# The last chunk of an FNet-and-GLU kernel: closing the sums one group early and making the last group in row form

## The chip, the cores and the metric

The kernel runs on one core of one Trainium2 chip. The metric is the device time of one execution in microseconds (us), lower is better. The profile's times are on one profiled execution's clock; its span runs from the first to the last instruction. The engines are PE (TensorE, with PEld for its weight loads), DVE (VectorE), ACT (ScalarE), POOL (GpSimd) and SP (SyncE, which here only issues DMAs).

## The reference

```python
# x: (8, 3008, 256) float32
X = np.fft.fft(x, axis=1)
X = np.fft.fft(X, axis=2)
y = X.real.reshape(8 * 3008, 256)

gate = 1.0 / (1.0 + np.exp(-(y @ w_gate)))      # w_gate, w_val: (256, 1536)
val = y @ w_val
out = gate * val @ w_out                        # w_out: (1536, 256), out: (24064, 256)
```

## The kernel before

The Fourier transform over the sequence is made with tables of cosines and sines, by folds of x on POOL and DVE and products on PE. The transform over the features is merged into the weights of gate and value (`G1`, `G2`). Rows k and S - k of a sequence come out of the same products, as sum and difference, so the main loop handles two mirrored rows at a time.

The main loop runs over batches (8), chunks of at most 252 row pairs (6 per batch, the last of 246), and the 12 blocks of 128 hidden features. One step of it is a slot: 576 slots. Three slots make a group, four groups a chunk; the last group has the number 191. In a slot, `front_a` and `front_b` make the gate and value products into a PSUM bank `pf`; `seed` and `part` put the middle feature in and take a copy; `gate_a` and `gate_b` apply the sigmoids and multiply, which leaves in `h` a tile of 128 hidden features by n row pairs, twice (for the row and its mirror). All of it is laid out with features on the partitions.

The product with `w_out` doesn't multiply plainly. It is a bilinear scheme that saves products: per group, three feature blocks, three thirds of the 2n rows and two halves of the 256 outputs are multiplied with 15 products instead of 18 (`PRODUCTS`), from sums of blocks of `h` (`sf`, made by POOL in `gate_b`, L653: 13 per group) and sums of blocks of `w_out` (`wf`, made once at the start). `back` issues the 15 products of a group in three parts of five, five slots behind the front; they add up over the four groups of a chunk in five PSUM banks, `PO`, three blocks of R = 2n/3 columns in each. As soon as a bank has its last product in the fourth group, it is copied to the tile `c` (L677, on ACT or DVE).

`finish` then forms the outputs: 20 sums of blocks of `c` (`C_SUMS` and `C_LAST`, line L700), DVE transposes in blocks of 32 by 32 (`flip`, L710), since here the output features are on the partitions, and stores in runs of 64 features, 256 bytes (`store`, L719 and L723). For an ordinary chunk these steps are put on a list, `later`, and are taken from it two or three per slot beside the next chunk. In the last chunk nothing follows: they come straight after the last product, six of the sums go to POOL, the blocks of the fifth bank are read from PSUM without a copy, and the 16 stores alternate between the queues of SP and ACT.

The order on each engine is that of the program text. DMAs are issued by SP and ACT in order, and an instruction that waits holds up what stands behind it in its queue.

At the start the weights are loaded into tiles that later serve other ends. The last four feature blocks of `w_out` pass through tile `x4`, which then takes x of the next batches (L148); `weight_join` (L310) on POOL is the last step of a weight's conversion, `forms` makes the blocks of `wf` from it. `mirror_x` copies x of the next batch into a mirrored layout in DRAM (`xr`; L160, L164, L169), and `e_rows` (L583) loads a broadcast row `ek` for each chunk.

Of the kernel before, what the change touches and what calls it, by code (L numbers as in the profile page):

```python
# [6 lines left out]

F32 = mybir.dt.float32
I32 = mybir.dt.int32
# [43 lines left out]
NQ = 6  # L53
# [23 lines left out]
OUT = (3, 12)  # L77
# [4 lines left out]
def kernel(  # L82
# [10 lines left out]
    nc = tc.nc  # L93
    B, _, _, _, D = xf.shape
    F = moe_w_gate.shape[1]
    P = 128
    S = out.shape[0] // B
    M = S // 2
    NK = M + 1
# [3 lines left out]
    NPR = NFT // 2  # L103
    NG = NFT // 3
    CH = 252
    NB = 1 + max(b // 3 for b in PLACE)
    WC = 256
    HD = D // 2
    TB = 32
# [9 lines left out]
    xp = ctx.enter_context(tc.tile_pool(name="xp", bufs=1))  # L119
    pqp = ctx.enter_context(tc.tile_pool(name="pqp", bufs=2))  # L120
    dram = ctx.enter_context(tc.tile_pool(name="dram", bufs=1, space=bass.MemoryType.DRAM))
# [5 lines left out]
    sp = ctx.enter_context(tc.tile_pool(name="sp", bufs=2))  # L127
    cp = ctx.enter_context(tc.tile_pool(name="cp", bufs=2))
    op = ctx.enter_context(tc.tile_pool(name="op", bufs=1))
# [3 lines left out]
    def mm(o, l, r, start, stop):  # L133
        nc.tensor.matmul(o, l, r, start=start, stop=stop, skip_group_check=True)  # L134

    def bank(name, other=None):
        if other is not None:
            return pso.tile([P, 512], F32, name=name, tag=f"po{other}")
        return psx.tile([P, 512], F32, name=name, tag="x")
# [46 lines left out]
    zero = dram.tile([2, 1, D], F32, name="zero")  # L186
    table = const.tile([2, 1], F32, name="table")
    ed = dram.tile([B, NK + 1], F32, name="ed")

    def load_table(t, nq):  # L190
        for q in range(0, NQ, nq):
            yield nc.sync.dma_start(out=ST[0][0:NP, t, q : q + nq], in_=stab[:, t, q : q + nq])
# [119 lines left out]
    WO, parts_ = {}, []  # L312

    def weight_use(j, other=None):
        w, c = jobs[j]
        if w == 2:
            WO[c] = WS.pop(j)
            for g in range(NG):
                if (3 * g + 2) // 2 == c:
                    parts_.extend(forms(g))  # L320
        else:
            merge(WS.pop(j), w, c, other)
# [244 lines left out]
    chunks = [(k0, min(CH, -(-(NK - k0) // 3) * 3)) for k0 in range(0, NK, CH)]  # L567
    assert NK <= chunks[-1][0] + chunks[-1][1] <= NK + 1 and NFT == 12
    groups = [(b, c, g) for b in range(B) for c in range(len(chunks)) for g in range(NG)]
    H, SF, EK = {}, {}, {}  # L570

    def cut(i):
        b, c, _ = groups[i // 3]
        k0, n = chunks[c]
        f = i % NFT
        return PQE[b], slice(k0, k0 + n), n, f, slice(f * P, (f + 1) * P)
# [41 lines left out]
    def front_b(i):  # L618
        (_, qk, *_), ks, _, _, fs = cut(i)
        for g in range(2):  # L620
            mm(PF[i][:, g], G2[:, g, fs], qk[:, ks], False, True)
# [15 lines left out]
    def block(p, i):  # L637

        R = 2 * chunks[groups[p][1]][1] // 3
        return H[p][:, i % 3, i // 3 * R : (i // 3 + 1) * R] if i < 9 else SF[p][:, i - 9, 0:R]  # L640

    def gate_b(i):

        n = cut(i)[2]
        p, fh = i // 3, i % 3
        z, h, pf = Z.pop(i), H[p], PF.pop(i)
        nc.vector.tensor_tensor(h[:, fh, 0:n], h[:, fh, 0:n], pf[:, 1], op=ALU.mult)  # L647
        nc.scalar.activation(pf[:, 0], z[:, 0], AF.Sigmoid)  # L648
        nc.vector.tensor_tensor(h[:, fh, n:], pf[:, 0], z[:, 1], op=ALU.mult)  # L649
        if fh == 1:  # L650
            SF[p] = sp.tile([P, 8, 2 * CH // 3], F32, name="sf", tag="sf")
        for dst, a, b, op in H_SUMS.get(fh, ()):
            nc.gpsimd.tensor_tensor(block(p, dst), block(p, a), block(p, b),  # L653
                                    op=(ALU.subtract, ALU.add)[op])
# [3 lines left out]
    C = {}  # L658

    def back(p, part):  # L660

        b, c, g = groups[p]
        n = chunks[c][1]
        R = 2 * n // 3
        last = p == len(groups) - 1
        if part == 0 and g == 0:
            PO[:] = [pso.tile([P, 2 * WC], F32, name=f"po{t}", tag=f"po{t}") for t in range(NB)]
        for at_, (hb, wb) in list(enumerate(PRODUCTS))[part * 5 : part * 5 + 5]:
            t, j = divmod(PLACE[at_], 3)
            mm(PO[t][:, j * R : (j + 1) * R], wf[:, g, wb], block(p, hb), g == 0 and at_ % 3 == 0,  # L670
               g == NG - 1)
            if g == NG - 1 and at_ % 3 == 2:
                if t == 0:
                    C[0] = cp.tile([P, 10 * WC], F32, name="c", tag="c")
                    nc.gpsimd.memset(C[0][:, 15 * R : 15 * R + 40], 0.0)
                if not (last and t == NB - 1):
                    (nc.vector.tensor_copy if t == 1 or t == 3 and not last else nc.scalar.copy)(  # L677
                        C[0][:, 3 * t * R : 3 * (t + 1) * R], PO[t][:, 0 : 3 * R])
        if part == 2:
            del H[p], SF[p]  # L680
            if g == NG - 1:
                finish(b, c, last)

    def finish(b, c, last):
        k0, n = chunks[c]
        R = 2 * n // 3
        more = k0 + n > NK
        nb = -(-n // TB)
        t = C.pop(0)
        queues = (nc.sync, nc.scalar) if last else (nc.sync,)  # L690
        os_ = []

        new = set()

        def sum_(dst, a, b, op, engine=nc.vector):

            there = lambda i: last and i >= 3 * (NB - 1) and i not in new
            v = [PO[NB - 1][:, (i - 3 * NB + 3) * R : (i - 3 * NB + 4) * R] if there(i) else
                 t[:, i * R : (i + 1) * R] for i in (a, b)]
            engine.tensor_tensor(t[:, dst * R : (dst + 1) * R], *v, op=(ALU.subtract, ALU.add)[op])  # L700
            new.add(dst)

        def flip(s, h):
            if not os_:

                full = (sp.tile([P, 8 * (2 * CH // 3)], F32, name="os", tag="sf") if last else
                        op.tile([P, NK + 1], F32, name="os", tag="os"))
                os_.append(full[:, 0 : 4 * WC].rearrange("p (s b h j) -> p s b h j", s=2, h=2, j=TB))
            c0 = OUT[h] * R + (n + more if s else 0)
            nc.vector.transpose(os_[0][:, s, 0:nb, h, :], t[:, c0 : c0 + nb * TB])  # L710

        def store(s):
            m, r0 = (min(n, M - k0), b * S + k0) if s == 0 else (
                n - (k0 == 0) - more, b * S + S - k0 - n + 1 + more)
            full = m // TB
            for a in range(4):
                ps = slice(a * TB, (a + 1) * TB)
                cs = slice(a * 2 * TB, (a + 1) * 2 * TB)
                queues[a % len(queues)].dma_start(  # L719
                    out=out[r0 : r0 + full * TB, cs].rearrange("(b t) d -> t b d", t=TB),  # L720
                    in_=os_[0][ps, s, 0:full].rearrange("p b h j -> p b (h j)"))
                if m > full * TB:
                    queues[a % len(queues)].dma_start(out=out[r0 + full * TB : r0 + m, cs],  # L723
                                      in_=os_[0][a * TB : a * TB + m - full * TB, s, full].rearrange(
                                          "p h j -> p (h j)"))

        def add(f):
            if last:
                f()
            else:  # L730
                later.append(f)
        for x, e in C_SUMS:
            if x[0] == 7:
                add(lambda: flip(0, 0))
                add(lambda: (flip(0, 1), store(0)))
            add(lambda x=x, e=e: sum_(*x, engine=(nc.vector, nc.gpsimd)[last and e]))
        add(lambda: sum_(*C_LAST))
        add(lambda: flip(1, 1))
        add(lambda: (flip(1, 0), store(1)))


# [61 lines left out]
    def at(i, *fs):  # L803
        side.setdefault(i, []).extend(fs)
# [14 lines left out]
    i0 = NFT  # L819
    count = 3 * len(groups)  # L820
# [16 lines left out]
    for b in range(B - 1):  # L837
# [17 lines left out]
        if b < B - 2:  # L855
            at(g0 + 1, lambda b=b: load_x(b + 2))
            for i, f in zip(calm(s0 if b else 3 * i0), mirror_x(b + 2)):
                at(i, f)

    for i in range(count):  # L860
        front_a(i)
        if N1 <= i < NFT:
            part(i)
        if i:
            gate_a(i - 1)
        if not N1 <= i < NFT:
            part(i)
        if i0 <= i + 1 < count:
            seed(i + 1)
        if i:  # L870
            gate_b(i - 1)
        todo = pre.pop(i, []) + use.pop(i, [])
        for f in [parts_.pop(0)] + todo if parts_ else todo + [lambda: parts_ and parts_.pop(0)()]:
            f()
        if i >= 5:
            back((i - 5) // 3, (i - 5) % 3)
        front_b(i)
        n = 3 if i >= count - 8 else 2 + i % 2
        for f in later[0:n]:
            f()  # L880
        del later[0:n]
        for f in side.pop(i, []):
            f()
# [55 lines left out]
```

## Time and profile before

| what | value |
|---|---|
| runs | 1955.82, 1955.66, 1949.49 us; median 1955.66 |
| span of the profiled execution | 1953.1 us (no other time of its own is given for it) |
| granted TensorE clock, mean | 0.995 |
| PE busy | 1915.7 us, 98% |
| DVE, ACT, POOL busy | 1457.9, 1332.5, 1598.4 us |
| chain that ended last, by engine | PE 92%, DVE 4%, DMA 2%, ACT 1% |
| chain from 1934 us on, by line | PE po L134 33.5%, DVE c L700 18.2%, DVE os L710 5.6%, PE pf L134 4.1%, ACT c L677 2.9% |

The table's shares of the chain say what the end of the program was waiting for, step by step back from its last instruction. All matrix products are recorded by one helper, L134; they are told apart by the tile that they write: `pf` for the gate and value products, `po` for the products with `w_out`. A matrix product in float32 shows as two instructions.

### The profile page before, as it was taken

The page shows a single profiled execution, that of the slowest core. Times are in us where ns is not written, and L with a number is a line of the kernel's source. Part 1 is how long each engine was busy: PE and PEld are TensorE (multiplying, and loading weights), DVE is VectorE, ACT ScalarE, POOL GpSimd, SP SyncE. Part 2 cuts the span into 40 slices and gives each one's busy share as a digit, 9 for nine tenths or more (in the row PEclk, how much of TensorE's full clock was granted, in tenths as well). Part 3 has the DMA queues.
Part 4 walks back from the last instruction along what each step waited for, and adds up shares of the span by engine and source line. Part 5 has one row for each costly group of instructions (what it writes and reads, how often), then busy time and mean ns, then how long its engine had stood idle before and what let it go on. Part 6 is the DMA issues. An engine that isn't in the chain of part 4 may idle for free.

```text
span 1953.1 us, 34554 instructions
## 1 busy us (share of the span) xinstructions
PE 1915.7 (98%) x11252; PEld 1788.2 (92%) x11252; DVE 1457.9 (75%) x3271; ACT 1332.5 (68%) x3122; POOL 1598.4 (82%) x2853
## 2 busy tenths in 40 slices
PE   6999999999999999999999999999999999999997
PEld 3789889999999999999999999999999999999997
DVE  5877787787777877777777777777777777777776
ACT  2567757776777677776777767777677766777775
POOL 3679998997889788997889869888789886777776
PEclk8999999999999999999999999999999999999999
DMA  9352513112012020212012021111200110011011
GB/s 268 91 134 20 117 32 111 46 25 82 14 46 58 16 79 14 60 46 79 14 25 80 16 79 25 45 51 21 83 17 14 22 20 14 14 22 20 14 20 27
DMA packets 169746, 96.78 MB, mean 50 GB/s; under 512 B 133858, under 2 KB 161636, under 8 KB 167020
## 3 DMA queue, kind: packets, MB, share of 16 engines
q1 hardware_dynamic: 167610, 94.06, 20.2%
q8 instruction: 90, 1.47, 0.3%
q10 hardware_dynamic: 1926, 0.52, 0.1%
q14 instruction: 88, 0.72, 0.1%
q0 software_dynamic: 32, 0.00, 0.0%
HBM read 69.83 MB, written 46.71 MB: 60 GB/s over the span
## 4 chain that ended last, share of the span: by engine, by line
PE 92%; DVE 4%; DMA 2%; ACT 1%; issue 0%; SPq 0%; POOL 0%; DVEq 0%; ACTq 0%; POOLq 0%
PE pf L134 48%; PE po L134 40%; PE ev L134 3%; DMA st<-in_stab_dram 1%; DVE c L700 1%; PE od L134 1%; DMA ge<-G 1%; PE ps L134 1%; DVE z L635 0%; ACT pf L648 0%; DVE h L649 0%; DVE h L647 0%; DVE ae L614 0%; DVE wf L370 0%; DMA raw<-in_moe_w_gate_dram 0%
## 5 line engine op out<-in xcount | busy, mean ns | idle before, releaser
L653 POOL TENSOR_TENSOR sf<-h 128x168 f32<-128x168 f32 (+1 forms) x960 | 533.3, 575 | 222.3 <-DVE h L649 222.3
L653 POOL TENSOR_TENSOR sf<-h,sf 128x168 f32<-128x168 f32 (+1 forms) x1152 | 645.1, 580 | 63.0 <-DVE h L649 62.6
L134 PE MATMUL pf<-qk,G 128*128 128x252 f32 (+1 forms) x2304 | 583.1, 376 | 4.3 <-DVE ae L614 2.4
L134 PE MATMUL pf<-pk,G 128*128 128x252 f32 (+1 forms) x2304 | 583.2, 376 | 1.5 <-DVE h L649 1.5
L649 DVE TENSOR_TENSOR h<-pf,z 128x252 f32<-128x252 f32 (+1 forms) x576 | 241.7, 420 | 425.0 <-ACT pf L648 425.0
L595 ACT ACTIVATE pf<-ek,ge 128x252 f32<-128x252 f32 (+1 forms) x1128 | 531.6, 471 | 18.6 <-DVE h L649 0.2
L134 PE MATMUL po<-sf,wf 128*128 128x168 f32 (+1 forms) x3072 | 529.9, 305 | 0.0
L611 ACT ACTIVATE ae<-pf 128x504 f32<-128x504 f32 (+1 forms) x569 | 335.5, 590 | 233.3 <-PE pf L134 232.3
L134 PEld LDWEIGHTS pf<-pk,G 128*128 128x128 f32 x2304 | 436.1, 190 | 55.3 <-DVE h L649 2.6
L134 PEld LDWEIGHTS po<-sf,wf 128*128 128x128 f32 x3072 | 472.7, 190 | 8.2
L134 PE MATMUL po<-h,wf 128*128 128x168 f32 (+1 forms) x2688 | 476.0, 305 | 0.2 <-DVE wf L367 0.2
L700 DVE TENSOR_TENSOR c<-c 128x168 f32<-128x168 f32 (+1 forms) x949 | 447.7, 504 | 5.5 <-ACT c L677 0.2
L134 PEld LDWEIGHTS po<-h,wf 128*128 128x128 f32 x2688 | 427.5, 190 | 17.2 <-DVE wf L367 0.6
L134 PEld LDWEIGHTS pf<-qk,G 128*128 128x128 f32 x2304 | 409.8, 190 | 31.9 <-ACT ae L611 3.2
L635 DVE TENSOR_TENSOR z<-ae,pf 128x504 f32<-128x504 f32 (+1 forms) x569 | 378.7, 666 | 23.4 <-ACT h L630 21.8
L630 ACT ACTIVATE h<-pf 128x252 f32<-128x252 f32 (+1 forms) x576 | 218.1, 379 | 156.3 <-PE pf L134 151.9
L648 ACT ACTIVATE pf<-z 128x252 f32<-128x252 f32 (+1 forms) x576 | 214.4, 372 | 114.8 <-DVE h L647 112.2
L647 DVE TENSOR_TENSOR h<-h,pf 128x252 f32<-128x252 f32 (+1 forms) x576 | 232.7, 404 | 0.0
L653 POOL TENSOR_TENSOR sf<-sf 128x168 f32<-128x168 f32 (+1 forms) x192 | 111.0, 578 | 15.1
L653 POOL TENSOR_TENSOR sf<-sf,h 128x168 f32<-128x168 f32 (+1 forms) x192 | 105.2, 548 | 0.0
L677 ACT COPY c<-po 128x504 f32<-128x504 f32 (+1 forms) x144 | 81.9, 569 | 2.6 <-PE po L134 2.6
L134 PE MATMUL ev<-st,x 63*128 63x189 f32 (+3 forms) x372 | 73.6, 348 | 10.2 <-DVE x L398 7.9
(138 smaller groups left out, 874.9 us busy)
## 6 DMA issues: line engine op xcount, KB each, us to landing
x<-xr SPq DMA_DIRECT2D x14, 1536.0 KB
out_dram<-os SPq DMA_DIRECT2D x380, 56.0 KB
xr<-in_xf_dram SPq DMA_DIRECT2D x14, 768.0 KB
xr<-in_xf_dram SPq DMA_DIRECT2D x35, 256.0 KB
ek<-ed SPq DMA_DIRECT2D x39, 126.0 KB
out_dram<-os SPq DMA_DIRECT2D x288, 7.0 KB
st<-in_stab_dram SPq DMA_DIRECT2D x4, 1111.9 KB
x<-in_xf_dram SPq DMA_DIRECT2D x2, 1512.0 KB
```

What stands on the lines that cost most here:

```text
L134: nc.tensor.matmul(o, l, r, start=start, stop=stop, skip_group_check=True)
L595: nc.scalar.activation(PF[i][:, g], EK[i // NFT], AF.Copy, scale=ge[:, g, f : f + 1])
L611: nc.scalar.activation(AP[i], PF[i], AF.Copy, scale=2.0)
L630: nc.scalar.activation(H[p][:, fh, 0:n], PF[i][:, 0], AF.Sigmoid)
L635: nc.vector.tensor_tensor(z[:, :, ::-1], AP.pop(i), PF[i], op=ALU.subtract)
L647: nc.vector.tensor_tensor(h[:, fh, 0:n], h[:, fh, 0:n], pf[:, 1], op=ALU.mult)
L648: nc.scalar.activation(pf[:, 0], z[:, 0], AF.Sigmoid)
L649: nc.vector.tensor_tensor(h[:, fh, n:], pf[:, 0], z[:, 1], op=ALU.mult)
L653: nc.gpsimd.tensor_tensor(block(p, dst), block(p, a), block(p, b), op=(ALU.subtract, ALU.add)[op])
L677: (nc.vector.tensor_copy if t == 1 or t == 3 and not last else nc.scalar.copy)(C[0][:, 3 * t * R : 3 * (t + 1) * R], PO[t][:, 0 : 3 * R])
L700: engine.tensor_tensor(t[:, dst * R : (dst + 1) * R], *v, op=(ALU.subtract, ALU.add)[op])
```

## The change

- **Closing early.** In the last chunk the 15 products are summed over three groups, 188 to 190, and closed with group 190 (`close = NG - 2`). The copies out of PSUM and the sums (`finish`) stand behind group 190's products. There are no transposes there any more; the summed tile is kept for `rows_out`.
- **The last group.** Group 191 makes no block sums on POOL. `rows_out` takes its three tiles of `h` as the stationary operand, in four tiles of rows (128 and 116 rows, and 128 and 117 of the mirrored side), and unscrambled `w_out` as the moving one: 12 products of 256 columns into four PSUM banks, with rows on the partitions.
- **Adding the sums.** Per row tile, two products with the summed tile as stationary operand and an identity matrix as the moving one (128 columns each) transpose the sums and add them in the same bank.
- **Storing.** Each row tile is copied out of PSUM (ACT, DVE, ACT, and the fourth half by each) and stored by one DMA with full rows of 1024 bytes, on SP and ACT in turn.
- **Where the weights come from.** At the start, when the last two loads of `w_out` have been converted, each is stored to DRAM (`wkeep`, 256 KB each, on SP, one ahead of the mirrored copies of x and one between them). In slot 540 `tail_load` loads them (512 KB) into the tile `x4`, which is free by then, and POOL makes the identity there.

The core of the diff:

```diff
+    wkeep = dram.tile([P, 4, D], F32, name="wkeep")
...
             WO[c] = WS.pop(j)
+            if c >= NPR - 2:
+                lo = 2 * (c - NPR + 2)
+                nc.sync.dma_start(out=wkeep[:, lo : lo + 2], in_=WO[c])
...
         nc.vector.tensor_tensor(h[:, fh, n:], pf[:, 0], z[:, 1], op=ALU.mult)
+        if p == len(groups) - 1:
+            return
         if fh == 1:
...
-        last = p == len(groups) - 1
+        last = p >= len(groups) - NG
+        close = NG - 2 if last else NG - 1
+        if p == len(groups) - 1:
+            rows_out(p, part)
+            return
...
-               g == NG - 1)
-            if g == NG - 1 and at_ % 3 == 2:
+               g == close)
+            if g == close and at_ % 3 == 2:
...
+    def tail_load():
+        full = xp.tile([P, 4 * NQ * D], F32, name="tail", tag="x4")
+        tail["w"] = full[:, 0 : 4 * D].rearrange("p (f d) -> p f d", f=4)
+        tail["one"] = full[:, 4 * D : 4 * D + P]
+        tail["os"] = full[:, 5 * D : 9 * D].rearrange("p (t d) -> p t d", t=4)
+        nc.sync.dma_start(out=tail["w"], in_=wkeep)
+        make_identity(nc, tail["one"])
+
+    def rows_out(p, part):
+
+        b, c, g = groups[p]
+        k0, n = chunks[c]
+        R = 2 * n // 3
+        m = M - k0
+        tiles = [(0, P), (P, m - P), (n + 1, P), (n + 1 + P, n - 1 - P)]
+        if part == 0:
+            tail["ps"] = [bank("row", 0 if i == 3 else None)[:, 0:D] for i in range(4)]
+
+        def direct(fs):
+            for (r0, rows), ps in zip(tiles, tail["ps"]):
+                for f in fs:
+                    mm(ps[0:rows], H[p][:, f, r0 : r0 + rows], tail["w"][:, 1 + f], f == 0, False)
+        direct(((0, 1), (2,), ())[part])
+        if part < 2:
+            return
+        t = C.pop(0)
+        queues = (nc.sync, nc.scalar)
+        for i, ((r0, rows), ps) in enumerate(zip(tiles, tail["ps"])):
+            out_ = ps.rearrange("p (a h j) -> p h a j", h=2, j=TB)
+            for h in range(2):
+                c0 = OUT[h] * R + r0
+                mm(out_[0:rows, h], t[:, c0 : c0 + rows], tail["one"].rearrange("p (a j) -> p a j", j=TB),
+                   False, h == 1)
+            os_ = tail["os"][0:rows, i]
+            if i < 3:
+                (nc.vector.tensor_copy if i % 2 else nc.scalar.copy)(os_, ps[0:rows])
+            else:
+                nc.scalar.copy(os_[:, 0:HD], ps[0:rows, 0:HD])
+                nc.vector.tensor_copy(os_[:, HD:], ps[0:rows, HD:])
+            row = b * S + (k0 + r0 if i < 2 else S - k0 - 2 * n + 1 + r0)
+            queues[i % 2].dma_start(out=out[row : row + rows], in_=os_)
...
         for x, e in C_SUMS:
-            if x[0] == 7:
+            if x[0] == 7 and not last:
...
         add(lambda: sum_(*C_LAST))
+        if last:
+            C[0] = t
+            return
...
+    at(count - 3 * i0, tail_load)
     for i in range(count):
         front_a(i)
```

The transposes and stores of `finish` keep one queue, SP, and one output tile, since only ordinary chunks use them now.

More of the change, by code (lines that the diff above doesn't have):

```diff
@@ L6 @@
 from concourse._compat import with_exitstack
+from concourse.masks import make_identity
 F32 = mybir.dt.float32
@@ L680, in back @@
             del H[p], SF[p]
-            if g == NG - 1:
+            if g == close:
                 finish(b, c, last)
+    tail = {}
+    def tail_load():
[36 more added lines that the diff above has]
+            queues[i % 2].dma_start(out=out[row : row + rows], in_=os_)
     def finish(b, c, last):
@@ L689, in finish @@
         t = C.pop(0)
-        queues = (nc.sync, nc.scalar) if last else (nc.sync,)
         os_ = []
@@ L704, in flip @@
             if not os_:
-                full = (sp.tile([P, 8 * (2 * CH // 3)], F32, name="os", tag="sf") if last else
-                        op.tile([P, NK + 1], F32, name="os", tag="os"))
+                full = op.tile([P, NK + 1], F32, name="os", tag="os")
                 os_.append(full[:, 0 : 4 * WC].rearrange("p (s b h j) -> p s b h j", s=2, h=2, j=TB))
@@ L718, in store @@
                 cs = slice(a * 2 * TB, (a + 1) * 2 * TB)
-                queues[a % len(queues)].dma_start(
+                nc.sync.dma_start(
                     out=out[r0 : r0 + full * TB, cs].rearrange("(b t) d -> t b d", t=TB),
@@ L722, in store @@
                 if m > full * TB:
-                    queues[a % len(queues)].dma_start(out=out[r0 + full * TB : r0 + m, cs],
+                    nc.sync.dma_start(out=out[r0 + full * TB : r0 + m, cs],
                                       in_=os_[0][a * TB : a * TB + m - full * TB, s, full].rearrange(
```

## The prediction

> **What bounds the kernel now.** I read the page first, then the chain of waits from 1934 us on, then the timeline of the same stretch, the waits of SP at the very end, and a table by stage of the start, where the change puts two stores.
>
> ```profile
> span 1953.1 us, 34554 instructions
> PE 1915.7 (98%) x11252; PEld 1788.2 (92%) x11252; DVE 1457.9 (75%) x3271; ACT 1332.5 (68%) x3122; POOL 1598.4 (82%) x2853
> ```
>
> TensorE is the bound over the whole span, and the change leaves its stream alone up to the last group. So nothing is to be won or lost before about 1935 us, except by a stall. What can move is the end, where the chain leaves PE:
>
> ```profile
> 1935.36 6.14 PE po L134 x44
> ...
> 1941.52 0.58 ACT c L677
> ...
> 1942.12 0.57 DVE c L700
> ...
> 1945.54 0.57 DVE c L700 x2
> 1946.11 0.68 DVE os L710 x2
> 1946.78 0.22 DVE c L700
> ...
> 1947.03 0.45 DVE os L710
> ```
>
> The chain waits for the products of group 191 on PE, then for a copy by ACT, the sums on DVE, and the transposes. The stores follow. The timeline has the durations (start, length, engine, line, operation):
>
> ```profile
> 1937.79 0.41 DVE L649 TENSOR_TENSOR h<-pf,z 128x246 f32<-128x246 f32 x1 [0.51 <-ACT pf L648]
> 1937.98 1.83 PE L134 MATMUL po<-h,wf 128*128 128x164 f32 x12
> 1939.02 0.57 ACT L677 COPY c<-po 128x492 f32<-128x492 f32 x1 [1.25 <-PE po L134]
> 1939.85 0.67 DVE L677 COPY c<-po 128x492 f32<-128x492 f32 x1 [1.64 <-PE po L134]
> 1940.21 2.11 PE L134 MATMUL po<-sf,wf 128*128 128x164 f32 x14
> 1940.63 1.25 DVE L700 TENSOR_TENSOR c<-c 128x164 f32<-128x164 f32 x3
> 1942.12 2.31 DVE L700 TENSOR_TENSOR c<-c 128x164 f32<-128x164 f32 x4 [0.24 <-ACT c L677]
> 1944.98 1.27 POOL L700 TENSOR_TENSOR c<-c 128x164 f32<-128x164 f32 x2 [0.74 <-DVE c L700]
> 1946.81 0.33 SPq L719 DMA_DIRECT2D out_dram<-os  x1
> 1950.80 0.28 SPq L723 DMA_DIRECT2D out_dram<-os  x1
> ```
>
> PE ends at 1942.3, the last sum at 1947.0, the last transpose at 1947.8, the last of 16 stores is issued at 1950.80, and the span ends at 1953.1. From the first copy waiting for PE (1939.85) to the end is 13.3 us, and only the part behind the h of 1937.79 can be shortened.
>
> **The change, part by part.** All times are on this execution's clock. The page gives no time of its own for the execution beside the span; 1953.1 is 2.6 under the median of the runs, 1955.66, and I move the sum over by that.
>
> *Start of the sums.* Group 190's 20 instructions start at 1935.20 and follow each other every 0.139, so its last bank is full at 1938.1. Now it closes the sums. Bank 0 is full before 1934, and its ACT copy (0.57) stands behind the sigmoid that ends at 1934.92: over at 1935.51, in a gap of 0.47 that ACT has there, so it pushes the next sigmoid by 0.1. DVE is busy until 1936.9 with z and absorbs that. The copies of banks 2 and 3 on ACT start when pf<-z ends (1937.76) and are over at 1938.9. The copy on DVE of bank 1 stands behind h: 1938.25 to 1938.92. Sums start at 1939.02 instead of 1940.63. The first three took 1.25 beside POOL's sums for h, which are gone (all 13 of the last group); alone, the later rows are 0.24 to 0.36 apart, so they take 0.95. The fourth starts at 1939.97, not 1942.12. From there to the 13th's end I keep the old 3.98, since POOL's first four sums run beside them as before: 1943.95, and the 14th ends at 1944.2 (before: 1947.0). POOL's last two end at 1944.1. Gain so far 2.8.
>
> *Products with h stationary.* Twelve of 256 columns take the place of 15 of 164. A product is two instructions; 252 columns take 0.2125 each, so 256 take 0.216, and twelve 5.18: 1937.98 to 1943.16. Their tile banks are free in time (pf of the last slot at 1938.2, before tile 2's first product at 1939.7). They lie beside the sums. The eight identity products of 128 columns are 0.217 each by the same rate; bounded from above by the narrowest shape shown here, 0.278. The first tile's second half waits for sum 11 (1943.7); the rest finds its sums ready. PE ends at 1945.5 (1946.0 by the upper bound) with the 0.17 of its pipe.
>
> *PSUM to store.* The four transposes (1.6 on DVE) go. A copy of 256 columns has no row; between the 0.38 of 246 and the 0.57 of 492 on ACT I take 0.39, on DVE 0.42. ACT: tile 0 until 1944.6, then the issue of tile 1's store (0.38, it waits for DVE's copy, 1945.05), behind which tile 2's copy is queued until 1945.9 and half of tile 3 until 1946.2. DVE's half waits for ACT: 1946.45. The last store is issued at 1946.5, 4.3 earlier than now. Stores go from 16 to 4, from runs of 256 B to rows of 1 KB.
>
> *Landing.* SP's last wait is for the last small store:
>
> ```profile
> SPq L935 <- DMA out_dram<-os: 0.8, 1, 0.8
> ```
>
> Issued at 1950.80 it is there at about 1952.0: 1.2, and 1.1 are left to the end of the span, which stay. The new last store has 117 KB instead of 5.2. Its transfer is bounded by two copies of 1 KB runs at the start:
>
> ```profile
> 112.00:114.00 2.00, 2.00 (x13) 1.84 (x12) 1.55 (x6) 1.57 (x7) 0.66 (x2) 1.00 0.82 292
> 116.00:123.00 7.00, 6.82 (x39) 6.16 (x39) 5.24 (x14) 5.34 (x13) 4.92 (x10) 1.00 0.27 97
> ```
>
> (last two columns: DMA share, GB/s.) The copy of 256 rows runs at 292, the mirrored ones, whose outer size is 4, at 97 with a quarter of the engines. 117 KB (119,800 bytes) take 0.4 or 1.2. I take 0.4: the store's outer size is 117, nearer to the first. By this the end is 1946.5 + 1.2 + 0.4 + 1.1 = 1949.2: 3.9, say 4.0, less. The Trainium skill (DMA: Bandwidth & Descriptors, Why a DMA increments its semaphore by 16 and not by 1) says that a DMA is spread over the largest number up to 16 that divides the outer sizes; the mirrored copies' quarter agrees. By it the 116 rows of tile 1 get 4 engines and the 117 of tile 3 get 13, which speaks against cutting rows this way. Tile 1 at 97 GB/s would land at 1945.1 + 1.2 + 1.2 = 1947.5, still ahead of tile 3 at 1948.1, so the sum stands.
>
> *Work elsewhere.* Two stores of 256 KB go on SP at about 101.4 and 104.3. The second waits for POOL's weight join, 108.17 to 109.46, with four mirrored copies, one row copy, the load of x and an ek load queued behind it. What covers that is the backlog: the row copy issued at 102.23 and the two mirrored ones before it keep the DMA engines busy until about 111 (768 KB at 292, then 2 x 256 KB at 97). So the load of x moves by the 2 x 0.9 us of its own transfer, from 126.6 to about 128.4; POOL reads x first at 157.17 and its packets ended at 137; ek, issued at 138.74, is read at 148.85. Without the backlog the delay is 5 us and ek still comes about 1 us early. The load of 512 KB and the identity (a fill and a select on POOL, at most 0.55 each by the 128x168 rows) stand in slot 540, near 1840, where POOL idles 1.5 to 2 us per group and SP between 1834 and 1860. Cost 0; without that cover 1.1 on POOL.
>
> **Rivals.** (1) *The gain is given back at the end.* The last store takes 97 GB/s and lands as late as the first big one now does (issued 1946.81, its queue slot free 1.8 later): 0.8 + 0.6 more, the identity products at their upper bound 0.5 more. Total gain 2.1. For it: rows of 1 KB from SBUF are not shown. Against: only four stores are under way.
>
> (2) *Weight loads come into the open; slower.* Each row product needs its own load of h, or of c, and a load is 0.19 (mean of its rows). If it ran ahead of its product rather than under the one before, the 40 instructions cost 40 x 0.19 = 7.6 more than forecast; less 0.4 of waiting for sums that it covers, PE ends at 1952.7 and the span is 1956.3, 3.2 longer. It decides from 0.1 per load on. Against: in the po stream a load of 0.190 and a product of 164 columns come every 0.139, so the load is hidden there. The Trainium skill (TensorE: Matmul & The Clock Gate, The mechanism) says that a load overlaps a running product only when the row groups differ, and here all use all rows; the trace contradicts it.
>
> (3) *The last store is narrow.* If 117 rows went through one engine, a quarter of 97, they would take 4.9: end at 1953.7, 0.6 slower. Against: nothing here shows fewer than four.
>
> (4) *The wait on SP at the start reaches TensorE*, through ek or x: back come 1 to 4 of the 4. Against: the covers above.
>
> That the change does something else than it says is excluded by the program's order: up to group 190 the engines' lists are the same but for the moved copy and the side work.
>
> **How the numbers follow.** Forecast (gain 2.8 to 5) 0.74, rival 1 0.12, rival 2 0.05, rival 3 0.03, rival 4 0.06. The forecast is 1955.66 - 4.0 = 1951.7. Every case lies within 0.5% (9.8 us), about what a measurement of this kernel can tell from no change. The runs themselves are 6.3 apart (1949.49 to 1955.82), more than the gain, so they make the range: 1949.49 less 4.5 gives 1945.0, 1955.82 with a slight loss (rival 3) gives 1956.4. A median at the lower level would stand just beyond 0.5% below: hence 0.07 for faster; 0.03 for slower, for a stall that no row shows; 0.90 for the same.
>
> **What would show it.** Right: the DVE copy at about 1938.3, the sums from 1939.0 to 1944.2, twelve row products back to back from 1938.0 (0.43 each), the last store's issue near 1946.5, span near 1949. Wrong: gaps of 0.1 or more between row products (rival 2), more than 2 us from the last issue to its landing (1, 3), x or ek awaited near 149 to 157 (4), or a POOL stall near 1840. If the sums end at 1944.2 and the span is still 1953, the stores have taken it.

## The result and the profile after

The changed kernel takes 1946.65 us in the median of 20 runs (1944.25 to 1952.3), the kernel before 1951.92 in 20 runs (1948.87 to 1957.78). The ratio is 0.9974, with a 95% interval of 0.9965 to 0.9984: 5.1 us less, between 3.1 and 6.8. The forecast was 4.0 less, which lies in this interval, and a median between 1945.0 and 1956.4, which held too. Its 1951.7 is 5 us above the measured median for another reason in the main: it was counted from the median of three runs, 1955.66, which is 3.7 above that of 20. The profiled execution's span is 1949.0 instead of 1953.1.

The page of the changed kernel, first two lines of numbers:

```profile
span 1949.0 us, 34556 instructions
PE 1917.7 (98%) x11262; PEld 1789.8 (92%) x11262; DVE 1461.0 (75%) x3269; ACT 1332.5 (68%) x3125; POOL 1589.7 (82%) x2842
```

PE is the bound as before. Its chain of waits from 1930 us on now goes from PE straight to the copies out of PSUM; no sum is on it (start, length, what):

```profile
1934.45 2.78 PE po L135 x20
1937.24 6.07 PE row L135 x32
...
1943.33 0.43 DVE tail L732
...
1943.79 0.27 ACTq L737
...
1944.37 0.28 ACT tail L734
...
1944.67 0.29 DVE tail L735
```

The timeline of the same stretch:

```profile
1933.46 0.99 PE L135 MATMUL pf<-qk,G 128*128 128x246 f32 x4
1936.87 0.41 DVE L654 TENSOR_TENSOR h<-pf,z 128x246 f32<-128x246 f32 x1 [0.51 <-ACT pf L653]
1937.07 5.34 PE L135 MATMUL row<-tail,h 128*128 128x256 f32 x24
1937.20 0.66 DVE L688 COPY c<-po 128x492 f32<-128x492 f32 x1
1937.90 2.90 DVE L754 TENSOR_TENSOR c<-c 128x164 f32<-128x164 f32 x7
1938.91 3.71 POOL L754 TENSOR_TENSOR c<-c 128x164 f32<-128x164 f32 x6 [6.40 <-DVE c L754]
1942.25 1.93 PE L135 MATMUL row<-tail,c 128*128 128x128 f32 x16
1942.38 0.31 DVE L754 TENSOR_TENSOR c<-c,po 128x164 f32<-128x164 f32 x1
1944.10 0.37 ACT L732 COPY tail<-row 128x256 f32<-128x256 f32 x1 [0.83 <-DVE tail L732]
1945.00 0.33 ACTq L737 DMA_DIRECT2D out_dram<-tail  x1
```

The copy by DVE follows h at once, the seven first sums run together, the row products come without a gap, and the last issue is at 1945.00. From there to the end of the span are 4.0 us, where the forecast had 2.7. A table by stage shows what fills them (last two columns: share of the 16 DMA engines and GB/s):

```profile
1944.00:1944.60 0.60, 0.18 (x2) 0.00 (x0) 0.00 (x0) 0.50 (x2) 0.00 (x0) 1.00 0.66 219
1944.60:1945.20 0.60, 0.00 (x0) 0.00 (x0) 0.29 (x1) 0.04 (x1) 0.00 (x0) 1.00 0.41 94
1945.20:1945.60 0.40, 0.00 (x0) 0.00 (x0) 0.00 (x0) 0.00 (x0) 0.00 (x0) 1.00 0.48 133
1945.60:1946.40 0.80, 0.00 (x0) 0.00 (x0) 0.00 (x0) 0.00 (x0) 0.00 (x0) 1.00 0.77 233
1946.40:1947.60 1.20, 0.00 (x0) 0.00 (x0) 0.00 (x0) 0.00 (x0) 0.00 (x0) 0.63 0.24 75
1947.60:1949.00 1.40, 0.00 (x0) 0.00 (x0) 0.00 (x0) 0.00 (x0) 0.00 (x0) 0.50 0.00 0
```

The first store (128 rows) is fast; as it ends, the rate falls to 94 GB/s, and with the store of 116 rows alone under way (1944.80 to 1945.15) the DMA share is 0.26, a quarter of the 16 engines, at 61 GB/s. The last 1.2 us of transfer, to 1947.6, go at 75. One more transfer falls into this stretch, a single packet of 16 KB that the profile lists as `instruction`, from 1945.15 to 1946.44:

```profile
q8 instruction: 1, 0.02, 1.3%
```

**A measure for the end.** Spans can't be compared directly, because the slots before the end come at other times in each execution: slot 575's first front product starts at 1934.37 before and at 1933.46 after. So 0.9 of the 4.1 us between the two spans has nothing to do with the last chunk. From that product to the end of the span it is 18.8 before and 15.6 after (1953.13 - 1934.37 and 1949.05 - 1933.46; the table is worked out from unrounded times). The end itself brought **3.2**. All experiments are read by this measure. Four executions with the old end gave 18.8 and 18.8 for the kernel before, 19.0 and 19.0 with the side work added: repeats agree within 0.1, but two programs with the same end can be 0.3 apart, so differences of 0.3 mean nothing. All times below with a plus sign count from that product.

| kernel | slot 575 at | last sum | PE's last product | last issue | end |
|---|---|---|---|---|---|
| before | 1934.37 | +12.6 | +8.0 | +16.4 | +18.8 |
| changed | 1933.46 | +9.2 | +10.7 | +11.5 | +15.6 |
| e1_even | 1931.74 | +9.3 | +10.7 | +12.7 | +15.6 |
| e2_one | 1928.66 | +9.3 | +10.7 | +12.5 | +19.1 |
| e3_short_runs | 1933.12 | +9.3 | +10.7 | +15.4 | +17.9 |
| e4_pool_sums | 1929.44 | +11.0 | +12.4 | +13.2 | +16.9 |
| e5_side_only | 1934.04 | +12.6 | +8.0 | +16.5 | +19.0 |
| e6_no_sums_added | 1931.94 | +9.3 | +9.0 | +12.5 | +15.2 |
| e7_even_sp | 1930.39 | +9.3 | +10.7 | +11.8 | +14.5 |
| e8_sp_only | 1929.62 | +9.3 | +10.7 | +11.4 | +15.1 |
| e9_sp_no_add | 1930.59 | +9.3 | +9.0 | +11.3 | +14.0 |
| e10_dve_copy | 1929.19 | +9.3 | +10.7 | +11.6 | +14.9 |
| e11_before_again | 1936.55 | +12.6 | +8.0 | +16.5 | +18.8 |
| e12_side_again | 1932.92 | +12.6 | +8.0 | +16.4 | +19.0 |

### The profile page after: what moved, and what is told of

Read it like the earlier page. It is cut to its first block, busy times and chain, and to the rows that moved or that the text cites. A ratio compares the mean times of both kernels' runs of the same rounds, so it can differ in the third digit from the quotient of the medians.

```text
span 1949.0 us, 34556 instructions
## 1 busy us (share of the span) xinstructions
PE 1917.7 (98%) x11262; PEld 1789.8 (92%) x11262; DVE 1461.0 (75%) x3269; ACT 1332.5 (68%) x3125; POOL 1589.7 (82%) x2842
## 4 chain that ended last, share of the span: by engine, by line
PE 92%; DVE 4%; DMA 2%; ACT 1%; issue 0%; SPq 0%; ACTq 0%; DVEq 0%
PE pf L135 48%; PE po L135 40%; PE ev L135 3%; DMA st<-in_stab_dram 1%; DVE c L754 1%; PE od L135 1%; DMA ge<-G 1%; PE ps L135 1%; DVE z L640 1%; ACT pf L653 0%; DVE h L654 0%; DVE h L652 0%; PE row L135 0%; DVE wf L375 0%; DMA raw<-in_moe_w_val_dram 0%
## 5 line engine op out<-in xcount | busy, mean ns | idle before, releaser
L660 POOL TENSOR_TENSOR sf<-h,sf 128x168 f32<-128x168 f32 (+1 forms) x1146 | 638.4, 576 | 61.5 <-DVE h L654 60.9
```

## Experiments on the landing: how wide is a store?

**Even stores.**

```diff
-            queues[i % 2].dma_start(out=out[row : row + rows], in_=os_)
+            for q0, q1 in [(0, rows)] if rows == P else [(0, 112), (112, rows)]:
+                queues[i % 2].dma_start(out=out[row + q0 : row + q1], in_=os_[q0:q1])
```

> The stores of 116 and 117 rows are cut into 112 + 4 and 112 + 5 rows; nothing else changes. Measure: from the first front product of slot 575 to the end of the span, 18.7 us before the change, 15.5 after it. Theory (the number of rows decides how many DMA engines a store runs on, and the 4-engine store holds up the one behind it on its queue): the last landing comes 1.2 to 1.7 after its issue instead of 3.0, less 0.35 for one more issue, so 14.3 to 14.8. Rival (rows of 1 KB out of SBUF land late in any case): 15.5 to 16.0.

Measured 15.6: a miss; as the rival said, and yet not for its reason. Tile 3's 112 rows, the last big store on ACT, landed 1.9 after their issue, against 3.0 for the 117 rows of the changed kernel, near the theory's 1.2 to 1.7; but the last issue of all, now tile 2's store on SP, came 1.1 later. SP's waits tell why:

```profile
SPq L738 <- DMA out_dram<-tail: 2.4, 1, 2.4
```

In the trace, tile 2's store and the 112-row store of tile 1 signal the same completion semaphore, the counter that is raised as a store's data lands: the 112 rows landed at +12.6, and tile 2's store was issued at +12.7. More stores had shifted the assignment. The run is therefore inconclusive as a time; e7 and e8 take its place.

**One engine.**

```diff
-            queues[i % 2].dma_start(out=out[row : row + rows], in_=os_)
+            for q0, q1 in [(0, 113), (113, rows)] if i == 1 else [(0, rows)]:
+                queues[i % 2].dma_start(out=out[row + q0 : row + q1], in_=os_[q0:q1])
```

> The store of 116 rows is cut into 113 + 3 rows; the other stores stay whole. 113 has no divisor up to 16 but 1. Theory (engines by divisor): 113 packets of 1 KB on one engine at about 0.05 us each take 5.7 us instead of 1.5, and the end waits for them: 15.5 + 3 to 4 = 18.5 to 19.5 us from the first front product of slot 575 to the end. Rival (the number of engines does not matter, or is not by divisor): 15.5 to 16.0.

Measured 19.1, as the theory said. SP's last wait in this run:

```profile
SPq L993 <- DMA out_dram<-tail: 5.6, 2, 5.4
```

The store of 113 rows, with the same bytes per row, was issued at 1939.00, and the long wait for it is over 7.4 us later. It was issued as early as the 116 rows in the changed kernel (+10.3). ACT's last issue came 0.9 later than there, behind the issue of the 3 rows, but that did not set the end. From +16.3 to +17.8 the trace has one packet after another, 0.042 apart: the rest of the 113 rows, and only then, from +17.4 on, the last packet of the 3 rows and nine of tile 3's 117. So a one-engine store holds up what stands behind it in its queue, and the rival falls.

The traces settle the number of engines directly. After a store's issue they hold the times of its completion signals. There are 16 for 128 or 112 rows, 13 for 117, 4 for 116 and 1 for 113; where there are fewer than 16, one more comes within 0.6 us of the issue. The number of engines goes by divisors of the row count.

**The queue alone, and the queue with even stores.** In e8 tile 1's store moves from ACT to SP, in whole rows; in e7 it moves and both odd stores are cut to 112 and the rest.

```diff
-            queues[i % 2].dma_start(out=out[row : row + rows], in_=os_)
+            (nc.scalar if i == 3 else nc.sync).dma_start(out=out[row : row + rows], in_=os_)
```

> The changed kernel with the store of tile 1 on SP, and whole stores of 116 and 117 rows: the last run (14.5 us from the first front product of slot 575) without its cut into 112 rows. Theory (the 4-engine store is what costs, whichever queue it is on; tile 2 now stands behind it on SP): 14.8 to 15.4. Rival (the queue was the cause, the cut did nothing): 14.4 to 14.6.

> The changed kernel with the stores cut into 112 + 4 and 112 + 5 rows, and those of tile 1 issued on SP, so that ACT's copies of tiles 2 and 3 no longer stand behind them. Theory (engines by divisor, and ACT held up 0.8 us by the issue that waits for DVE): 1.3 to 2.0 us less than the changed kernel, 13.5 to 14.2 from the first front product of slot 575; against the kernel before 0.9960 to 0.9972. Rival (landing and issue order do not matter): as the changed kernel, 15.5, 0.9974.

Measured 15.1, within the theory's range, and 14.5, a miss by 0.3. Moving tile 1's store away from ACT's queue went with 0.5 less, cutting both odd stores evenly with another 0.6. Of the 0.5, only 0.16 is an earlier issue (+11.5 to +11.4, since ACT's copies must wait for PE anyway), and the rest is not shown to be the queue's. Below, e4 has the stores and queues of the changed kernel and takes 3.7 from its last issue to the end, as little as e8 (3.8), where the changed kernel took 4.0. That difference is itself within the scatter. What the traces show to differ there is the `instruction` packet. In the changed kernel 12 of the last store's 13 signals came by +13.9 and the last at +14.6. In all four changed kernels with such a packet among the stores (the changed kernel, e1, e2, e8) some store has a last signal that comes 0.5 to 1.2 behind the one before it; in e4, e6, e7, e9 and e10, which have none there, the last one lags by 0.24 at most. This fits an engine that was busy with the packet, but no run tests it.

That even stores land sooner is better supported. From the issue of the last store of 112 or 117 rows to its last signal it is 1.9, 2.0, 1.9 and 2.2 in e1, e7, e9 and e10 (112 rows), and 2.4, 2.7 and 3.0 in e4, e8 and the changed kernel (117). Each of the two steps is at most twice the scatter of 0.3; the two together, 1.1, are well beyond it. Against the kernel before, e7 was timed at 0.9975 (0.9961 to 0.9989). That is above the range expected too, and can't be told from the changed kernel's 0.9974: 1 us is 0.05%.

**Short runs.** Every row tile in four stores of 64 columns:

```diff
-            queues[i % 2].dma_start(out=out[row : row + rows], in_=os_)
+            for q0 in range(0, D, 64):
+                queues[q0 // 64 % 2].dma_start(out=out[row : row + rows, q0 : q0 + 64], in_=os_[:, q0 : q0 + 64])
```

> Each row tile is stored in four DMAs of 64 columns, runs of 256 bytes as before the change, in turn on SP and ACT; nothing else changes. Theory (few stores of full rows are part of the gain): 12 more issues at 0.4 on two queues, some of them ahead of ACT's copies, and four times the packets on the 4 engines of the 116-row tile: 17.0 to 18.5 us from the first front product of slot 575 to the end, against 15.5. Rival (only the earlier issue counts, bytes are bytes): 15.5 to 16.3.

Measured 17.9, as the theory said; the last issue came 3.9 later (+15.4), held up by stores that waited for earlier ones to land:

```profile
SPq L738 <- DMA out_dram<-tail: 6.5, 3, 5.8
```

So 2.3 of the change's 3.2 hang on its four whole stores. The number of stores costs, through their issue and through the shared semaphores that they wait for.

## Experiments on the sums: who sets the end of the row products?

**POOL's sums put back.**

```diff
         nc.vector.tensor_tensor(h[:, fh, n:], pf[:, 0], z[:, 1], op=ALU.mult)
-        if p == len(groups) - 1:
-            return
```

> The 13 block sums of the last group are put back on POOL; nobody reads them. Theory (POOL's freedom is part of the gain: its share of the output sums starts at 1938.9 only because these are gone): POOL starts its output sums 1.7 us later, DVE's seventh sum waits for the first of them, and the span from the first front product of slot 575 grows from 15.5 to 16.7 to 17.3. Rival (the sums have room beside the row products, PE sets the end): 15.5 to 16.0.

Measured 16.9, within the theory's range. POOL begins its output sums 2.0 later by this measure, and PE, which has no wait at the end of the changed kernel, now has one:

```profile
PE row L135 <- DVE c L752: 1.4, 1, 1.4
```

The last issue came 1.7 later and the end 1.3, so 1.3 of the gain or somewhat more hangs on the 13 block sums that fell away. This and the 2.3 of the whole stores were each measured alone and don't add up. No run closes the sums early without the row form, or has the row form without closing early, so what each half of the change brings stays open.

**The identity products left out.** The row products then close their banks themselves.

```diff
-                    mm(ps[0:rows], H[p][:, f, r0 : r0 + rows], tail["w"][:, 1 + f], f == 0, False)
+                    mm(ps[0:rows], H[p][:, f, r0 : r0 + rows], tail["w"][:, 1 + f], f == 0, f == 2)
...
-            for h in range(2):
-                c0 = OUT[h] * R + r0
-                mm(out_[0:rows, h], t[:, c0 : c0 + rows], tail["one"].rearrange("p (a j) -> p a j", j=TB),
-                   False, h == 1)
```

> The eight identity products that add the sums of three groups are left out, so the output holds the last group alone; the sums are still formed. Theory (the end of PE's row products sets the end, the sums are hidden): the copies start 1.75 us earlier, except that DVE's copy of tile 1 stands behind the last sum (1942.7), so 0.6 to 1.2 us less: 14.3 to 14.9 from the first front product of slot 575. Rival (the sums set the end): 0 to 0.2 less, 15.3 to 15.5.

> Cut stores, all six on SP, and the eight identity products left out, so the output holds the last group alone; no store shares a completion semaphore with another that is under way. Reference: 14.5 with the products. Theory (PE's row products set the end, the sums end some 0.6 earlier than they would have to): 0.3 to 0.6 less, 13.9 to 14.2, since DVE's copy of tile 1 then waits for the last sum. Rival 1 (the sums have far more room): 1.7 less, 12.8. Rival 2 (the sums set the end): 14.4 to 14.6.

In e6 PE ended 1.76 earlier (+9.0), but the end came only 0.3 earlier, at 15.2, outside both ranges: again two stores shared a semaphore, and the second one on SP was issued at +12.5. e9 avoids that by putting all six even stores on SP: 14.0 against e7's 14.5, as its theory said. (In e7 tile 3's two stores are on ACT, so the 0.5 holds that move as well.) The identity products cost 1.76 on PE and about 0.5 at the end, because the last sum (+9.3) and DVE's copy of tile 1 behind it come next. In the changed kernel the sums end 1.5 before PE does: they are hidden, with little to spare.

**A shorter way out.** Tile 3 copied by DVE alone, its 5 rows on SP:

```diff
-            if i < 3:
+            if True:
                 (nc.vector.tensor_copy if i % 2 else nc.scalar.copy)(os_, ps[0:rows])
-            else:
-                nc.scalar.copy(os_[:, 0:HD], ps[0:rows, 0:HD])
-                nc.vector.tensor_copy(os_[:, HD:], ps[0:rows, HD:])
...
-            queues[i % 2].dma_start(out=out[row : row + rows], in_=os_)
+            for q0, q1 in [(0, rows)] if rows == P else [(0, 112), (112, rows)]:
+                (nc.scalar if i == 3 and q0 == 0 else nc.sync).dma_start(out=out[row + q0 : row + q1], in_=os_[q0:q1])
```

> Cut stores, tile 1 on SP, tile 3 copied by DVE in one piece instead of half by ACT and then half by DVE, its 5 rows on SP. Theory (what lies between PE's last product and the last issue counts in full): 0.3 to 0.5 less than 14.5, 14.0 to 14.2; against the kernel before 0.9960 to 0.9976. Rival (the landing hides it): 14.4 to 14.6.

Measured 14.9, and 0.9978 (0.9967 to 0.9989) against the kernel before. This was a miss: DVE's copy was indeed over earlier, but the 5 rows came last on SP (+11.6), and 1.8 passed from the last packet to the end, where e7 had 1.5. The 0.4 between the two is little more than the scatter. None of the versions is shown to beat the changed kernel in its runs; e7 does by the trace of its end.

## Experiments on the start: side work and scatter

> The kernel before with the side work alone: the two stores of 256 KB at the start, the load of 512 KB in slot 540 and the identity on POOL, which nobody reads. Theory (covered by the DMA backlog and by slack): no difference beyond 0.1 per cent, the load of x issued within 2 us of 126.6, no wait of PE for it. Rival (the wait on SP reaches TensorE): 1 to 4 us slower. A third (the 0.9 us by which slot 575 came earlier in the profile after the change is from the side work): 1 us faster, slot 575 at 1933.5 instead of 1934.4.

The edit is the kernel before with the two stores, `tail_load` and the identity added. Measured 0.9996 (0.9982 to 1.0011): no difference that the runs can tell, though the interval, 3.5 us less to 2.1 us more, leaves room for the lower part of the rival's 1 to 4. The traces go further: the load of x is issued at 126.45 in e5 and at 126.75 in the changed kernel, against 126.58, and between 95 and 200 us PE's longest wait is for DVE and much the same (2.4 us in e5, 2.3 after the change, 2.4 before), with none for x or `ek`. The wait of SP that the prediction named is there, in the changed kernel's waits:

```profile
SPq L322 <- POOL wx L312: 4.5, 1, 4.5
```

but nobody needs what stands behind it in that time. The two instructions on POOL cost 0.20 and 0.29.

> The kernel before, once more under the profiler, to see where executions of one program differ. Theory (they differ in the first 60 us, before the stream on PE is closed, and the end is the same): slot 575 anywhere from 1928 to 1935 us, and 18.7 to 18.9 from it to the end. Rival (the change itself brought slot 575 forward): slot 575 at 1934.0 to 1934.8 again.

> The kernel with the side work alone and the old end, a second time under the profiler. Up to slot 540 its program is that of the changed kernel. So far slot 575 was reached at 1934.0 to 1936.6 in three executions with the old end and at 1928.7 to 1933.5 in ten with the new one. Theory (the first 60 us vary from one execution to the next, whatever stands at the end): anywhere from 1928.5 to 1936.5, with 18.8 to 19.1 from there to the end. Rival (the old end goes with a late start, for a reason that is not known): 1934 or later.

Slot 575 was reached at 1936.55, later than e11's range, and at 1932.92, within e12's. The end of both was the old one, +18.8 and +19.0. So the time to slot 575 differs by 2.2 us (before, e11) and 1.1 us (e5, e12) between executions of one program. The difference arises at the start. The first front product comes at 58.1 us in the first profile, 59.5 in e11, 57.3 in e5, 55.9 in e12, and at 52.4 to 57.5 in the ten with the new end, while from there to slot 575 all fourteen take 1875.7 to 1877.2. At the start tables, weights and x are loaded, and from 3 to 45 us the DMA share is 0.92 and more in the four executions in which it was read (before, e12, after, e2). What stays open: the four executions with the old end reached slot 575 at 1932.9 to 1936.6, the ten with the new end at 1928.7 to 1933.5. Their ranges only overlap a little, though the programs are the same up to there but for the side work, which e5 and e12 have as well. Of the 5.1 us that the runs show, 3.2 are accounted for at the end; the interval begins at 3.1. Whether the remaining 1.9 is chance, or an earlier start that somehow goes with the new end, these runs don't decide. They were also taken on several chips. On one, the first front product came at 59.5 with the old end (e11) and at 52.5 to 53.7 with the new one (e8, e9, e10); on another, at 57.3 (e5) and at 57.5 and 54.4 (e3, e7).

## Why the prediction was right, step by step

One reading was wrong without effect: the first copy that waits for PE is ACT's of 1939.02, not DVE's of 1939.85, so from it to the end are 14.1 us and not 13.3. No term of the sum uses it.

- **Start of the sums: right in kind, too late by 0.2.** Forecast +4.65 (1939.02), measured +4.4. The copy by DVE stood behind h, as said; the copy of bank 0 on ACT pushed nothing.
- **End of the sums: too late by 0.6.** Forecast +9.8, measured +9.2. The fourth sum on DVE ran before POOL had started (0.32 instead of the 0.55 that I had kept), the rest of it is the earlier start. e4 shows that POOL's freedom mattered.
- **Row products: right.** 24 instructions at 0.216 and 16 at 0.11. PE ended at +10.7 (forecast +11.1); it did not wait for sum 11, which came earlier than forecast. PE, not the sums, sets the time at which the copies start.
- **Rival 2, weight loads in the open: excluded.** In the groups by tile, a load takes as long as before and the products are no further apart:

```profile
L135 PEld LDWEIGHTS row<-tail,c x16: 180/186/192, 1942.0 to 1943.8; 128*128 128x128 f32 x8, 128*116 128x116 f32 x4, 128*117 128x117 f32 x4
L135 PE MATMUL row<-tail,c x16: 272/273/275, 1942.3 to 1943.9; 128*128 128x128 f32 x8, 128*116 128x128 f32 x4, 128*117 128x128 f32 x4
```

  16 products start within 1.66 us, 0.11 apart, each with a load of 0.186 of its own. The loads run under the products, also for 128 columns.
- **Copies and last issue: too late by 0.6.** Forecast +12.1, measured +11.5, carried over from PE's earlier end. ACT's wait for DVE before its issue was there: the 0.83 in the timeline.
- **Landing: the term that was mis-sized.** I had 1.6 from the last issue to the landing and 2.7 to the end; measured 3.0 and 4.0. By the prediction's own sign (more than 2 from the last issue to its landing) this step was wrong. The 116 rows were cut down to 4 engines in the prediction and landed at +13.2, as forecast (+13.1); it is the last store, the 117 rows, that came late, at +14.6 instead of +13.7. The runs show that the row count is part of it: with 112 rows the last of these stores landed 1.9 to 2.2 after its issue, with 117 rows 2.4 to 3.0, and with 113 rows on one engine the end is 3.5 longer (e2). They don't show that standing on ACT's queue behind the 116 rows costs anything, since e4 ends as soon after its last issue as e8 does, on the same queues as the changed kernel. In the changed kernel's profile one late engine, beside the `instruction` packet, accounts for some 0.4 as well. And 112 rows still took 0.3 to 0.6 more than forecast, with other stores under way; what part each of these has stays open. The trace agrees with what the Trainium skill states (DMA: Bandwidth & Descriptors, Why a DMA increments its semaphore by 16 and not by 1), that a DMA is spread over the largest number up to 16 that divides its outer sizes: 13 completion signals for 117 rows, 4 for 116, 1 for 113.
- **Rival 1** had its place right, the landing, and the size of that part: 0.8 + 0.6 later, measured 1.3. Its reason was not right, since the last store ran on 13 engines and not on a quarter of them, and the 0.5 that it added for the identity products didn't come. So the end gained 3.2, between its 2.1 and the forecast.
- **Side work: right.** Nothing reached PE, by PE's waits in the traces and, within its interval, by e5.
- **The sum.** 4.0 was forecast and 4.1 found in the spans, but that agreement is luck: the end brought 3.2, and 0.9 came from an earlier slot 575. The 3.2 itself holds two errors of opposite sign: the last issue came 0.6 earlier than forecast, and what stands behind it took 1.3 longer.

## What to carry to other kernels

When work at the end of a program is cut, count back from the last store's landing, and count how each store is spread: 112 or 128 rows went over 16 engines, 117 over 13, 116 over 4 and 113 over one, and the one-engine store held up the next store on its queue. Few whole stores beat many short ones at the end, where nothing hides their issue; look also at whether two stores share a completion semaphore. And compare ends from a common instruction, since the spans of two executions can differ by more at the start than the change is worth.

## What was not expected of the hardware

- A store of 113 rows of 1 KB, 116 KB, had one completion signal from its data and took 7.4 us from issue to the end of the wait for it, while in e7 the stores with 112 rows let the last packet land 1.3 after the last issue.
- Executions of one program came to the same instruction at 1932.9 and 1934.0 (e12, e5), or at 1934.4 and 1936.6 (before, e11), while the 18.8 to 19.0 us behind it hardly varied.
- A packet of 16 KB that the profile lists as `instruction` took 1.29 us on the DMA engines while the last two stores of the changed kernel were under way.
- Sums on DVE took 0.32 each while POOL was idle, and 0.47 to 0.54 beside POOL's sums, in the same run and with the same shape.
